# Sixteen phase-scaled copies of the values: from VectorE to GpSimd

## The chip, the cores and the metric

The kernel runs on one core of one Trainium2 chip. The metric is the time of one execution in device microseconds (us); where several runs are given, their median. The core has five engines that take their own instructions in their own order and wait for each other by semaphores: TensorE (PE, matrix products; its weight loads are listed apart as PEld), VectorE (DVE), ScalarE (ACT), GpSimd (POOL) and SyncE (SP, which here issues most of the DMAs).

## The reference, cut to what matters

A sequence of 2048 tokens of width 448 goes through two branches, and a gate mixes them.

```python
x = A_x                                         # 1 x 2048 x 448, bf16
g = sigmoid((x * gate_w).sum(-1, keepdims=True))
# branch a: attention with 16 heads of 28
q, k, v = split(x @ wqkv)
p = softmax(einsum("bhqd,bhkd->bhqk", q, k) * 28 ** -0.5)
a = merge(einsum("bhqk,bhkd->bhqd", p, v)) @ wo
# branch b: a filter in the two-dimensional spectrum
b = irfft2(rfft2(B_x) * (w_r + 1j * w_i))
out = g * a + (1 - g) * b
```

The change touches only the attention, and in it only the values that one part of the softmax weights is multiplied with.

## The kernel before, in words

The 16 heads are handled as four groups `g` of four heads. The 2048 queries are cut into four chunks `c` of 512, the 2048 keys into 16 tiles `kt` of 128. So there are 16 stages, one for each pair of a group and a chunk; their order is groups 0 and 1 chunk by chunk, then groups 2 and 3 in turn. In a stage, each key tile gives a score block of 128 keys by 512 queries for each of four heads, and the exponentials of that block have to be made and multiplied with the values.

There are two ways to the exponentials. Most key tiles go through ACT: PE writes the scores to `psA` or `psB`, ACT writes their exponential into `ring` (L1034), PE multiplies `ring` with the values `vw` into the accumulator `pvb`. The last three to five key tiles of a stage (two in the very first), 69 over the kernel, go another way, called d below: PE writes the scores to a `bg` bank, DVE adds a constant and writes 16-bit whole numbers whose bits, read as bf16, are close to the exponential (L993, four instructions for four heads, into one `pd` buffer). POOL makes three more versions of that buffer, each with another whole number added to all bits (L1003, INT64_ADD, one instruction for each version, into another `pd` buffer). The four versions are four phases of the same approximation, and their mean is a better exponential. PE multiplies each of the four with its own copy of the values, `vd`, and adds all of them into `pvb`. Nine `pd` buffers go round; a new version can only be written when PE has read what the buffer held.

The copies `vd` take out what the phases added: for each phase `f` the values of the tiles concerned, with a column of weights, are multiplied by the constant `PHGAIN[f]`. That is the line of this change. For each group the source is `vt` (f32, 20 blocks of 29 numbers on each partition, written by DVE at L879 and POOL at L826), and four instructions on L888 write the four copies in bf16, sixteen in all. They stand in `v_block`, and what reads them is listed in `vdready`. Each group has its copies made shortly ahead of its first stage; groups 0 and 2 share one `vd` buffer, groups 1 and 3 the other.

In the background of the attention PE, DVE and SP carry the spectral branch and the projections of the next groups.

The order of all this is no scheduler's choice at build time. Every piece of work is recorded as an operation with an engine, and a packed table (`TABLE`, unpacked in `Sched.run`) lists the operations in the order in which they are emitted. Each engine gets its own instructions in that order. The duration and due time that are given with an operation are not read when the order comes from the table.

Two more things bear on the lines touched. An operation of DVE that is recorded with `lk=True` is followed by a note (`ported`), and `pin` then makes the next GpSimd instruction wait for that DVE instruction. And the program that is built names, ahead of GpSimd instructions of some kinds, a library that these need: an instruction without a tile's name, shown as `ISA` in the order. In the kernel before there is one of these ahead of L1003, at the first INT64_ADD.

Of the kernel before, what the change touches and what calls it, by code (L numbers as in the profile page):

```python
# [21 lines left out]
S, D, H, DH, F = 2048, 448, 16, 28, 225  # L22
# [106 lines left out]
def free_dims(ap, dims, offset=0):  # L129
    return _AP(tensor=ap.tensor, offset=ap.offset + offset,  # L130
               ap=[list(ap.ap[0])] + [list(d) for d in dims])
# [16 lines left out]
def dv(n, rate=1):  # L148
    return 0.067 + n / 960.0 / rate
# [138 lines left out]
class Kernel:  # L288
# [544 lines left out]
    def v_block(self, g, b, due, wop, rel=0.0):  # L833
        self.sc.ctx = ("v_block", g, b)
        nc = self.nc
        it = Item()
        ops = []
        W = self.wv0 if g == 0 else self.wvr
        o0 = 0 if g == 0 else self.WV0[g]
        m = 113 if g == 0 else 112  # L840
        for t in range(4):
            for c in range(4):
                n = CH[c]

                def f(t=t, c=c, n=n):
                    self.mm(self.bgi(it)[:, m * t:m * t + m], self.xT[b][0:n, c, 128 * t:128 * t + 128],
                            W[0:n, c, o0:o0 + m], c == 0, c == 3)
                deps = [self.xev[b, cc] for cc in range(4)] + self.wvd[g] + [wop[0]]
                ops.append(self.pe(112, f, deps + ops[-1:], due - 1.5, dur=0.052, acq=it if not ops else None, rel=rel))
        last = []  # L850
        if g == 0:
            def fg():
                self.pin(nc.vector.tensor_copy(out=self.glog[:, 4 * b:4 * b + 4],
                                               in_=free_dims(self.bgi(it), [[m, 4]], 112)))
            last = [self.dve(0.08, fg, ops[-1:], due - 1.5)]
            self.glops.append(last[0])
        tl = range(4 * b, 4 * b + 4)
        nv = len([t for t in tl if any(t in self.ak[self.nidx[g, c]] for c in range(4))])
        dl = [t for t in tl if any(t in self.dk[self.nidx[g, c]] for c in range(4))]
        d0 = dl[0] if dl else None  # L860
        vr = [wop[1]]
        if nv:
            def fe():
                src = free_dims(self.bgi(it), [[m, nv], [DH, 4], [1, DH]])
                wv = free_dims(self.w[g][:], [[4, nv], [1, 4], [0, DH]], 16 * b)
                self.pin(nc.vector.tensor_tensor(out=free_dims(self.vw[g][:], [[128, nv], [32, 4], [1, DH]], 4 * b * 128),
                                                 in0=src, in1=wv, op=ALU.mult))
            last = [self.dve(dv(112 * nv), fe, [ops[-1], wop[0], self.vms[g], ("vwar", g)] + last, due - 1.5,
                             free=None if dl else it)]
            vr.append(last[0])  # L870
        nd = len(dl)
        if nd:
            o = d0 - NT + DKT

            def fd():
                src = free_dims(self.bgi(it), [[m, nd], [DH, 4], [1, DH]], m * (d0 - 4 * b))
                wv = free_dims(self.w[g][:], [[4, nd], [1, 4], [0, DH]], 4 * d0)
                dst = free_dims(self.vt[:], [[4 * (DH + 1), nd], [DH + 1, 4], [1, DH]], 4 * (DH + 1) * o)
                self.pin(nc.vector.tensor_tensor(out=dst, in0=src, in1=wv, op=ALU.mult))  # L879
            last = [self.dve(dv(112 * nd), fd, [ops[-1], wop[0]] + self.vtr + last, due - 1.4, free=it)]  # L880
            self.vtw.setdefault(g, []).extend([last[0]] + [self.vdw[g, t] for t in dl])
        if b == 3 and self.vtw.get(g):
            t0 = min(t for c in range(4) for t in self.dk[self.nidx[g, c]])
            n4, o4 = 4 * (NT - t0), t0 - NT + DKT
            rd = []
            for f in range(4):
                def fs(f=f):
                    self.pin(nc.vector.tensor_scalar(  # L888
                        out=free_dims(self.vd[g][:], [[32, n4], [1, DH + 1]], 128 * (DKT * f + o4)),
                        in0=free_dims(self.vt[:], [[DH + 1, n4], [1, DH + 1]], 4 * (DH + 1) * o4),  # L890
                        scalar1=PHGAIN[f], scalar2=None, op0=ALU.mult))
                rd.append(self.dve(dv(n4 * (DH + 1), 2), fs, [self.vdms[g], ("vdwar", g)] + self.vtw[g], due - 1.3, lk=True))
            self.vtr = rd
            for t in range(t0, NT):
                self.vdready[g, t] = [[x] for x in rd]
        self.vready[g, b] = vr
# [574 lines left out]
```

## Time and profile before

| | |
|---|---|
| time, median of 3 runs | 380.67 us (380.51 to 381.52) |
| the profiled execution | 380.98 us |
| its span | 379.2 us |
| PE busy | 371.3 us (98%) |
| ACT busy | 351.1 us (93%) |
| DVE busy | 339.1 us (89%) |
| POOL busy | 234.4 us (62%) |

The profile is of one execution. A row of a group of instructions gives the line, the engine, the operation, the output and the input by the names in the program without buffer numbers, and how often it ran; then the busy time and the mean of one; then how long the engine stood idle just before them and what ended that. A row of a timeline gives the start, the length, the same names, and in brackets the idle time ahead of it and what released it. Rows whose engine ends in q (POOLq, SPq) are of the engine's own sequencer: waits, DMA issues, settings. Busy times of PE are partly modelled, so that 98% isn't PE at its peak.

### The profile page before, as it was taken

The page shows a single profiled execution, that of the slowest core. Times are in us where ns is not written, and L with a number is a line of the kernel's source. Part 1 is how long each engine was busy: PE and PEld are TensorE (multiplying, and loading weights), DVE is VectorE, ACT ScalarE, POOL GpSimd, SP SyncE. Part 2 cuts the span into 40 slices and gives each one's busy share as a digit, 9 for nine tenths or more (in the row PEclk, how much of TensorE's full clock was granted, in tenths as well). Part 3 has the DMA queues.
Part 4 walks back from the last instruction along what each step waited for, and adds up shares of the span by engine and source line. Part 5 has one row for each costly group of instructions (what it writes and reads, how often), then busy time and mean ns, then how long its engine had stood idle before and what let it go on. Part 6 is the DMA issues. An engine that isn't in the chain of part 4 may idle for free.

```text
span 379.2 us, 12643 instructions
## 1 busy us (share of the span) xinstructions
PE 371.3 (98%) x5117; PEld 142.4 (38%) x5117; DVE 339.1 (89%) x665; ACT 351.1 (93%) x389; POOL 234.4 (62%) x264
## 2 busy tenths in 40 slices
PE   8999999999999999999999999999999999999996
PEld 6634223342433333234333434233333323433564
DVE  1768899999999999999999999999999999988744
ACT  2799999999999999999999999999999999999841
POOL 4446465866778866565553565778597778483510
PEclk9999999999999999999999999999999999999999
DMA  6511101010210112211322212223222122222132
GB/s 145 157 34 44 29 18 36 4 36 2 41 52 22 44 41 54 55 38 30 68 60 93 69 40 49 57 61 70 45 64 74 30 69 72 86 64 72 35 103 75
DMA packets 31158, 21.23 MB, mean 56 GB/s; under 512 B 16260, under 2 KB 29052, under 8 KB 31100
## 3 DMA queue, kind: packets, MB, share of 16 engines
q1 hardware_dynamic: 29708, 19.96, 20.7%
q8 instruction: 40, 0.66, 0.7%
q10 hardware_dynamic: 1392, 0.46, 0.5%
q14 instruction: 18, 0.15, 0.1%
HBM read 14.51 MB, written 1.96 MB: 43 GB/s over the span
## 4 chain that ended last, share of the span: by engine, by line
PE 55%; ACT 31%; issue 6%; DVE 4%; DMA 2%; POOL 1%; SPq 0%; DVEq 0%; ACTq 0%; POOLq 0%
ACT ring L1034 31%; PE bg L432 24%; PE pvb L432 17%; PE psA L432 7%; PE psB L432 6%; DVE pd L993 2%; PE bg L435 1%; DMA CS<-cCS 1%; DVE X L1419 1%; POOL pd L1003 1%; DMA Wg<-in_B_w_i_dram 0%; DVE X L1298 0%; DVE q L1178 0%; DVE t L1362 0%; DVE wpq L1224 0%
## 5 line engine op out<-in xcount | busy, mean ns | idle before, releaser
L1003 POOL INT64_ADD pd<-pd x207 | 211.9, 1038 | 96.7 <-DVE pd L993 27.4
L1034 ACT ACTIVATE ring<-psA 128x1024 bf16<-128x1024 f32 x187 | 201.7, 1078 | 4.7 <-PE psA L432 3.2
L1034 ACT ACTIVATE ring<-psB 128x1024 bf16<-128x1024 f32 x187 | 201.7, 1079 | 2.6 <-PE psA L432 1.4
L993 DVE TENSOR_SCALAR pd<-bg 128x512 uint16<-128x512 f32 x276 | 180.9, 681 | 8.5 <-PE bg L432 3.5
L432 PE MATMUL pvb<-pd,vd 128*32 128x512 bf16 x1104 | 96.9, 384 | 0.1
L432 PE MATMUL bg<-q,k 32*128 32x512 bf16 x276 | 96.3, 383 | 0.2
L432 PEld LDWEIGHTS <-k 32*128 32x128 bf16 x1024 | 40.1, 91 | 122.4 <-issue 117.7
L432 PE MATMUL psB<-q,k 32*128 32x512 bf16 x374 | 73.2, 383 | 1.3 <-ACT ring L1034 0.7
L432 PE MATMUL psA<-q,k 32*128 32x512 bf16 x374 | 72.8, 383 | 0.5 <-ACT ring L1034 0.2
L432 PE MATMUL pvb<-ring,vw 128*32 128x512 bf16 x748 | 67.9, 384 | 0.0
L432 PEld LDWEIGHTS <-vd 128*32 128x32 bf16 x1104 | 25.3, 94 | 35.5 <-issue 31.1
L432 PEld LDWEIGHTS <-vw 128*32 128x32 bf16 x748 | 17.5, 94 | 22.7 <-issue 20.5
L432 PEld LDWEIGHTS <-xT 128*128 128x128 bf16 (+5 forms) x512 | 20.3, 97 | 10.7 <-issue 9.7
L432 PE MATMUL bg<-xT,wpq 128*32 128x512 bf16 (+3 forms) x244 | 21.2, 383 | 0.1
L1362 DVE TENSOR_TENSOR t<-bg,Wg 128x450 bf16<-128x450 f32 x32 | 18.8, 614 | 0.6 <-DMA Wg<-in_B_w_i_dram 0.4
L432 PE MATMUL bg<-xT,wpk 128*32 128x512 bf16 (+2 forms) x240 | 18.9, 383 | 0.0
L432 PE MATMUL bg<-wvr,xT 128*128 128x112 bf16 (+2 forms) x192 | 13.7, 213 | 0.0
L1178 DVE TENSOR_TENSOR q<-pvs,Rb 128x512 bf16<-128x512 f32 x15 | 10.9, 729 | 2.6 <-DMA Rb<-rsc 2.6
L1298 DVE TENSOR_TENSOR X<-bg,oc 128x226 bf16<-128x226 f32 (+1 forms) x32 | 12.3, 386 | 0.5
L432 PEld LDWEIGHTS <-CS 128*32 128x32 bf16 x384 | 9.0, 95 | 9.9 <-issue 5.6
L432 PE MATMUL bg<-xtok,CS 128*32 128x225 bf16 (+1 forms) x192 | 11.2, 294 | 0.7 <-DMA CS<-cCS 0.7
L742 DVE TENSOR_SCALAR k<-bg 128x512 bf16<-128x512 f32 x15 | 10.3, 685 | 1.3 <-PE bg L432 1.1
(117 smaller groups left out, 315.4 us busy)
## 6 DMA issues: line engine op xcount, KB each, us to landing
Rb<-rsc SPq DMA_DIRECT2D x60, 64.0 KB
CS<-cCS SPq DMA_DIRECT2D x16, 192.0 KB
V<-xtok SPq DMA_DIRECT2D x16, 113.0 KB
Wg<-in_B_w_i_dram SPq DMA_DIRECT2D x64, 28.1 KB
xtok<-Ab SPq DMA_DIRECT2D x16, 112.5 KB
xtok<-in_A_x_dram SPq DMA_DIRECT2D x3, 448.0 KB
Wg<-in_B_w_r_dram SPq DMA_DIRECT2D x32, 28.1 KB
out_dram<-wpq SPq DMA_DIRECT2D x6, 112.0 KB
```

The source lines that it names most:

```text
L432: self.pin(self.nc.tensor.matmul(out, lhsT=lhsT, rhs=rhs, start=start, stop=stop, **kw))
L435: self.pin(self.nc.tensor.transpose(out=out, in_=in_, identity=self.c("ident")[0:n, 0:n]))
L742: self.pin(nc.vector.tensor_scalar(out=dst, in0=self.bgi(it), scalar1=SQ, scalar2=None, op0=ALU.mult))
L993: self.pin(nc.vector.tensor_scalar(out=ys[:, s, :].bitcast(U16), in0=self.bgi(it), scalar1=127 * UNITS, scalar2=0.0, op0=ALU.add, op1=ALU. ...
L1003: self.pin(nc.gpsimd.int64_add(out=fl(pds), in0=fl(ys), in1=PHASE[f] * 0x0001000100010001))
L1034: self.pin(nc.scalar.activation(out=self.ring[:, u0:u0 + len(st), :], in_=slot[:, 0:len(st), :], func=ACT.Exp, scale=LN2 / UNITS))
L1178: e = self.dve(dv(512), lambda: self.pin(nc.vector.tensor_tensor(out=dst, in0=pvs[:], in1=self.Rb[:], op=ALU.mult)), ds, kk, lk=True)
L1298: self.pin(nc.vector.tensor_tensor(out=free_dims(self.X1[:, t, :], [[F, 2], [-1 if dif else 1, n]], (F - 1) * dif), in0=free_dims(self.bgi ...
L1362: self.pin(nc.vector.tensor_tensor(out=out[:], in0=self.bgi(it)[:, 0:F2].rearrange("p (a f) -> p a f", a=2), in1=free_dims(Wg[:], [[F, 2], ...
L1419: self.pin(nc.vector.tensor_tensor(out=free_dims(self.zt[0:FN], [[128, 4], [1, 128]], 512 * t), in0=self.bgi(it)[0:FN, :].rearrange("p (a ...
```

## The change

The sixteen instructions on L888 are issued on GpSimd in place of VectorE. They are recorded with a duration of 0.9 in place of one worked out for VectorE, and without the note that makes the next GpSimd instruction wait for them. The table of the order is the same, so each of the sixteen stands at the same place in the common order and therefore at a place in GpSimd's queue that the table gave to it for VectorE.

```diff
             for f in range(4):
                 def fs(f=f):
-                    self.pin(nc.vector.tensor_scalar(
+                    self.pin(nc.gpsimd.tensor_scalar(
                         out=free_dims(self.vd[g][:], [[32, n4], [1, DH + 1]], 128 * (DKT * f + o4)),
                         in0=free_dims(self.vt[:], [[DH + 1, n4], [1, DH + 1]], 4 * (DH + 1) * o4),
                         scalar1=PHGAIN[f], scalar2=None, op0=ALU.mult))
-                rd.append(self.dve(dv(n4 * (DH + 1), 2), fs, [self.vdms[g], ("vdwar", g)] + self.vtw[g], due - 1.3, lk=True))
+                rd.append(self.pool(0.9, fs, [self.vdms[g], ("vdwar", g)] + self.vtw[g], due - 1.3))
```

Three pieces of the order show what this does to the queues. In them a name such as `pd_113` is a tile with its number, `x2` means that two such instructions follow each other, and `L1003 ISA` with tiles is the INT64_ADD. An `ISA` without tiles sets the library: in the built program the one at L888 names library 0, the one at L1003 library 1.

GpSimd, at the copies of group 0, shortly before PE first reads them:

```order
 L533 COPY wpk_79<-X_131 96x8x28
-L1003 ISA pd_113<-pd_111 128x1024
+L888 ISA
+L888 TENSOR_SCALAR vd_116<-vt 128x20x29 x2
+L1003 ISA
+L1003 ISA pd_113<-pd_111 128x1024
+L888 ISA
+L888 TENSOR_SCALAR vd_116<-vt 128x20x29 x2
+L1003 ISA
 L1003 ISA pd_114<-pd_111 128x1024
```

Four copies came into the queue in two pairs with one INT64_ADD between them, and four settings of the library with them.

GpSimd, at the copies of group 3, whose first stage is the tenth:

```order
 L1003 ISA pd_113<-pd_110 128x1024
-L1003 ISA pd_111<-pd_110 128x1024
-L1003 ISA pd_107<-pd_115 128x1024
+L888 ISA
+L888 TENSOR_SCALAR vd_117<-vt 128x20x29 x3
+L1003 ISA
+L1003 ISA pd_111<-pd_110 128x1024
+L1003 ISA pd_107<-pd_115 128x1024
+L888 ISA
+L888 TENSOR_SCALAR vd_117<-vt 128x20x29
+L1003 ISA
 L1003 ISA pd_107<-pd_114 128x1024
```

Three copies and one, with two INT64_ADD between them. Over the kernel there are nine such clusters (two for group 0, three for group 1, two each for groups 2 and 3), and each brings one setting to library 0 and one back to library 1: eighteen more than before. In one cluster of group 1 a small cast (`vw`, L817) stands between the copy and the way back.

VectorE, at the copies of group 0:

```order
 L993 TENSOR_SCALAR pd_115<-bg_64 128x512
-L888 TENSOR_SCALAR vd_116<-vt 128x20x29
 L903 TENSOR_SCALAR ge<-ge 128x16
 L993 TENSOR_SCALAR pd_115<-bg_66 128x512
-L888 TENSOR_SCALAR vd_116<-vt 128x20x29
 L993 TENSOR_SCALAR pd_115<-bg_64 128x512
 L742 TENSOR_SCALAR k_89<-bg_65 128x512
-L888 TENSOR_SCALAR vd_116<-vt 128x20x29 x2
 L993 TENSOR_SCALAR pd_115<-bg_64 128x512
```

The copies left VectorE's queue and the rest closed up. The order of PE, ACT and SP is the same in both programs.

## The prediction

> **What bounds the kernel now.** I read the page first, then who waits for the lines touched, then the places in the trace where GpSimd would get its new work.
>
> ```profile
> PE 371.3 (98%) x5117; PEld 142.4 (38%) x5117; DVE 339.1 (89%) x665; ACT 351.1 (93%) x389; POOL 234.4 (62%) x264
> PE 55%; ACT 31%; issue 6%; DVE 4%; DMA 2%; POOL 1%; SPq 0%; DVEq 0%; ACTq 0%; POOLq 0%
> L1003 POOL INT64_ADD pd<-pd x207 | 211.9, 1038 | 96.7 <-DVE pd L993 27.4 <-PE pvb L432 12.6 <-PE psA L432 9.3
> ```
>
> PE and ACT feed each other without a gap and carry 86% of the chain that ended last. POOL has 1% of it and stands idle for 38% of the span. That suggests room on POOL, but the share is a mean; what counts is how far ahead of PE each INT64_ADD is done. I paired the 207 INT64_ADD with the products that read their buffers (by the buffers' numbers in the order). At the places concerned it looks like this, POOL's instruction first, then its reader:
>
> ```profile
> 48.44 5.10 POOL L1003 INT64_ADD pd<-pd  x5 [1.48 <-DVE pd L993]
> L432 PE MATMUL pvb<-pd,vd x4: 379/379/379, 50.7 to 50.7; 128*32 128x512 bf16 x4
> 105.09 1.04 POOL L1003 INT64_ADD pd<-pd  x1 [0.27 <-PE bg L432]
> L432 PE MATMUL pvb<-pd,vd x8: 379/384/390, 106.6 to 106.8; 128*32 128x512 bf16 x8
> 219.51 4.08 POOL L1003 INT64_ADD pd<-pd  x4 [0.40 <-PE pvb L432]
> L432 PE MATMUL pvb<-pd,vd x8: 379/379/379, 221.8 to 222.0; 128*32 128x512 bf16 x8
> 237.00 2.05 POOL L1003 INT64_ADD pd<-pd  x2 [0.86 <-PE pvb L432]
> L432 PE MATMUL pvb<-pd,vd x4: 389/390/390, 239.9 to 239.9; 128*32 128x512 bf16 x4
> ```
>
> One INT64_ADD takes 1.04 us. The first of the five at 48.44 is done at 49.48 and read at 50.7: a lead of 1.2 us. At 105.09 it is 0.7 us (read by the last four products, 106.8), at 219.51 1.45 us (222.0), at 237.00 1.9 us. So POOL is just in time. PE takes its instructions in a fixed order, so a late buffer stops not one product but everything behind it, the scores for ACT included; PE, 98% busy, has nothing to catch up with. Delay of POOL beyond idle time and lead goes into the time one for one.
>
> **The change part by part.**
>
> *Removed from VectorE.* Sixteen instructions of 0.47 us.
>
> ```profile
> L888 DVE TENSOR_SCALAR vd<-vt x16: 398/454/645, 38.5 to 236.2; 128x580 bf16<-128x580 f32 x16
>   POOL pd L1003: 8.2, 5
>   POOL vw L817: 2.5, 1
> ```
>
> Between them they are 7.2 us of VectorE. The two rows under the first list who waited for them: only POOL, 10.7 us in six places; those waits go with the notes. PE and ACT never waited for them, and L888 isn't in the chain. Ends: a gain of 7.2 us and nothing; I take nothing, since VectorE has 4% of the chain and POOL, not VectorE, is what these places will wait for.
>
> *Added to GpSimd: the copies.* No row has this operation there. The nearest are of other kinds:
>
> ```profile
> L661 POOL MEMSET vd<- 128x2560 bf16 x2 | 4.5, 2231 | 1.4 <-DVE sq L747 1.4
> 17.77 0.25 POOL L817 CAST vw<-w 128x16 bf16<-128x16 f32 x1
> 104.35 0.46 POOL L817 CAST vw<-w 128x64 bf16<-128x64 f32 x1 [2.53 <-DVE vd L888]
> 14.16 0.37 POOL L530 COPY wpq<-X 128x224 bf16<-128x224 bf16 x1 [2.39 <-DMA X<-in_A_wqkv_dram]
> ```
>
> The memset makes 0.87 ns an element; the two casts, which write scattered elements, differ by 0.21 us for 48 elements, 4.4 ns each. So 580 elements cost between 0.5 and 2.7 us. The copy with 224 elements in runs of 28 is nearest in layout (the new one has runs of 29): with a fixed part of 0.18 us, what the small cast has beyond its 16 elements, it makes 0.85 ns an element, and 580 come to 0.67 us. Sixteen: 10.7 us (the high end adds 33).
>
> *Added to GpSimd: eighteen changes of library.* This is the large term, and the trace before shows one such change:
>
> ```profile
> L1003 POOLq MODIFY_POOL_CONFIG  x2: 1/1/1, 32.5 to 32.5; - x2
> 32.06 0.37 POOL L626 MEMSET wvr<- 1x336 bf16 x1
> 33.27 1.04 POOL L1003 INT64_ADD pd<-pd  x1 [0.83 <-DVE pd L993]
> DMA packets 0, 0.00 MB, mean 0 GB/s; under 512 B 0, under 2 KB 0, under 8 KB 0
> ```
>
> Two records at 32.5 us, and the first INT64_ADD starts 0.83 us after the memset, a gap that is put down to VectorE. So here a change costs between nothing and 0.83 us. But the last row, of the stretch 32.4 to 33.3 us, says that no byte was moved meanwhile. Every earlier execution ended with this same library in use, so perhaps nothing had to change. In the changed kernel each of the eighteen names the other library than the one in use. If its code has to come from memory, the nearest rows are loads from memory that an engine stood waiting for, and the one row in which an engine takes in a table:
>
> ```profile
> 1.17 2.78 ACTq L407 DMA_DIRECT2D X<-in_A_wqkv_dram  x4
> 4.87 0.21 DVE L533 COPY wpq<-X 96x224 bf16<-96x224 bf16 x1 [4.87 <-DMA X<-in_A_wqkv_dram]
> 10.47 1.24 SPq L407 DMA_DIRECT2D X<-in_A_wqkv_dram  x2
> 3.98 1.28 ACT L575 ACT_TABLE_LOAD   x1 [3.98 <-issue]
> ```
>
> From the start of the issue to the reader's start: 1.17 to 4.87, and 10.47 to POOL's 14.16 (quoted above), both times 3.7 us. A change that is a load and then an installing costs 3.7 + 1.3 = 5.0 us, an estimate; two loads in series, one for each of the two records, 7.4 us. Ends: 0 and 7.4. I take 5.0, since a change that really changes something is nearer to a load than to the row in which no byte moved.
>
> The Trainium skill (GPSIMD Engine Reference, Instruction dispatch) says that the first call to a freshly loaded kernel also pays a load of about 6 us, measured between this same record and the first instruction behind it, without an instruction in the profile. The row at 32.5 us disagrees, with 0.83 us at most; by 5.95 us a change the sum below would be 492 us.
>
> *What hides it.* POOL's idle time at the nine places. The windows are those ahead of the clusters of group 0 (two), group 1 (the first), and groups 2 and 3 whole:
>
> ```profile
> 38.59:40.51 1.92, 1.92 (x27) 0.60 (x22) 1.60 (x5) 1.92 (x3) 0.00 (x0) 1.00 0.27 98
> 41.55:42.70 1.15, 1.15 (x19) 0.25 (x11) 1.15 (x4) 1.15 (x3) 0.00 (x1) 1.00 0.00 0
> 101.83:104.35 2.52, 2.52 (x36) 0.96 (x34) 2.52 (x8) 2.52 (x4) 0.00 (x0) 1.00 0.18 37
> 211.45:215.79 4.34, 4.31 (x62) 1.88 (x59) 4.34 (x12) 4.34 (x6) 1.04 (x1) 1.00 0.35 78
> 232.17:237.00 4.83, 4.81 (x65) 1.43 (x57) 4.80 (x12) 4.83 (x7) 2.05 (x2) 1.00 0.15 29
> sum 14.76, PE 14.70 PEld 5.12 DVE 14.40 ACT 14.76 POOL 3.09; mean PE 2.94 PEld 1.02 DVE 2.88 ACT 2.95 POOL 0.62
> 113.44 2.05 POOL L1003 INT64_ADD pd<-pd  x2 [1.10 <-DVE vd L888]
> 116.98 2.05 POOL L1003 INT64_ADD pd<-pd  x2 [1.08 <-DVE pd L993]
> ```
>
> That is 14.76 - 3.09 = 11.7 us, and in group 1 another 0.27 (at 105.09), 1.10 and 1.08: 14.1 us. The leads above can be used up once for each group: 5.2 us. Behind a late POOL the next wait is PE's for `pvb<-pd,vd`, and behind PE ACT's for `psA` and `psB`.
>
> The sum: 18 x p + 10.7 - 14.1 - 5.2 = 18 x p - 8.6, with p the price of one change; 5.0 gives 81 us.
>
> *PE after a stall.* Nine stalls of some 81 / 9 = 9 us each. Before, PE never stops that long, so the price of a restart is bounded by its first microseconds:
>
> ```profile
> 1.10 4.24 PE L432 MATMUL bg<-zero 128*128 128x256 bf16 x19 [1.10 <-POOL zero L509]
> 7.24 0.81 PE L432 MATMUL bg<-xT,wpq 128*128 128x512 bf16 x3
> ```
>
> At first 256 columns take 0.21 us (19 starts within 4.24 less one length of 0.42); from 7.24 on 512 columns take 0.21 us. So PE begins at half speed for at most 6 us and loses at most 2.8 us. Nine times: 0 to 25 us. I take the middle, 13, since nothing before shows whether a stall of 9 us brings the slow start back. The Trainium skill (TensorE: Matmul & The Clock Gate, Part 1) says that an idle window of about 3.4 us does, and that as long of activity ends it; at half speed that is 1.7 us a stall, 15 us in place of 13.
>
> **Result.** 380.98 us (span 379.2, 1.8 around it; 0.3 above the median 380.67) + 81 + 13 = 475 us.
>
> **Rivals.** *Cheap changes (0.8 to 1.3 us).* For it: the one change shown has a gap of 0.83 us; if a change costs what the table load does, 1.28. Against it: nothing was moved there. 18 x 0.83 - 8.6 = 6 us, 18 x 1.28 - 8.6 = 14: 387 to 395 us, without PE's restarts, as the stalls are too short.
>
> *Not slower.* If a change is only its two records, the copies alone, 10.7 us, fit in the 14.1 us of idle time that they inherit, and the note's waits are gone. It decides at p = 8.6 / 18 = 0.48 us: below that the time stays 381, or falls by up to 1 us if VectorE's relief reaches the chain. Against it: eighteen changes at 0.48 us or less need both libraries to lie ready beside each other.
>
> *Dear changes.* Two loads in series, 7.4 us: 18 x 7.4 - 8.6 + 25 = 150, 531 us. For it: two records for each change. Or copies at 2.7 us each.
>
> **How the numbers follow.** The forecast, that each change is a real load, has 0.62, with a range of its own from 439 us (3.7 us, no slow restarts) to 505 (6 us, all of them). Cheap changes 0.20, not slower 0.08, dear 0.10. The range 386 to 508 leaves out the last two. A measurement of this kernel can tell about 0.3% from no change: faster 0.03, within it 0.05, slower 0.92.
>
> **What would show it.** Eighteen more pairs of MODIFY_POOL_CONFIG; behind each a gap on POOL of about 5 us, in which it waits for nothing shown; nine stretches around 40, 105 to 120, 215 and 237 us with PE and ACT idle; L888 on POOL at about 0.67 us; outside of these stretches, the same lengths as before. The prediction is wrong if the gaps behind the records are under 1.3 us, or if PE runs on during them.

## The result, and the profile after

The changed kernel takes 511.2 us (median of 3 runs, 510.55 to 514.49) where the kernel before takes 380.67 us: 1.345 times as long (95% interval 1.341 to 1.349). The direction was forecast, the size was not: 475 us, with a range that ended at 508. The profiled execution took 510.55 us, 129.6 us more than the one before.

The page of the changed kernel, busy time of the engines, the rows of 40 slices for PE, POOL and PE's clock, the chain, and the groups touched:

```profile
span 508.8 us, 12680 instructions
PE 396.4 (78%) x5117; PEld 144.4 (28%) x5117; DVE 337.2 (66%) x649; ACT 355.7 (70%) x389; POOL 261.1 (51%) x280
PE   8993099999471629999999307952399999999997
POOL 5452156759242258656543225342287688776520
PEclk9997569999866659999999756575689999999999
PE 55%; issue 19%; POOL 11%; ACT 7%; DVE 6%; DMA 1%; SPq 0%; POOLq 0%; DVEq 0%; ACTq 0%
L1003 POOL INT64_ADD pd<-pd x207 | 211.8, 1036 | 139.9 <-issue 46.8
L432 PE MATMUL pvb<-pd,vd 128*32 128x512 bf16 x1104 | 107.4, 421 | 105.2 <-POOL vd L888 57.2
L888 POOL TENSOR_SCALAR vd<-vt 128x580 bf16<-128x580 f32 x16 | 26.9, 1684 | 62.7 <-issue 55.1
```

POOL's share of the chain went from 1% to 11%, and "issue" from 6% to 19%: time in which an engine waits for nothing that the profile shows. On POOL such time stands ahead of the two lines that a change of library precedes: 55.1 us ahead of L888, 46.8 us ahead of L1003. PE now stands ahead of `pvb<-pd,vd` for 105.2 us; the same row of the kernel before has 0.1 us in that place:

```profile
L432 PE MATMUL pvb<-pd,vd 128*32 128x512 bf16 x1104 | 96.9, 384 | 0.1
```

In the row of the slices of the changed kernel PE shows the places, the slices around 45 to 65, 130 to 190, 285 to 310 and 335 to 370 us: the four groups. Elsewhere PE is as full as before.

The first of these places in POOL's timeline, and the same stretch on PE:

```profile
38.20 0.37 POOL L533 COPY wpk<-X 96x224 bf16<-96x224 bf16 x1
45.48 3.44 POOL L888 TENSOR_SCALAR vd<-vt 128x580 bf16<-128x580 f32 x2 [6.91 <-issue]
54.76 1.03 POOL L1003 INT64_ADD pd<-pd  x1 [5.83 <-issue]
62.53 3.44 POOL L888 TENSOR_SCALAR vd<-vt 128x580 bf16<-128x580 f32 x2 [6.74 <-issue]
71.81 2.05 POOL L1003 INT64_ADD pd<-pd  x2 [5.83 <-issue]
```

```profile
47.24 0.62 PE L432 MATMUL pvb<-pd,vd 128*32 128x512 bf16 x4 [4.94 <-POOL vd L888]
64.29 0.62 PE L432 MATMUL pvb<-pd,vd 128*32 128x512 bf16 x4 [16.43 <-POOL vd L888]
```

Over the kernel each way to library 0 leaves a gap of 6.7 to 7.1 us on POOL, each way back 5.7 to 6.0 us; typical values are 6.9 and 5.85. Each pair of copies takes 3.44 us. PE waits 4.94 us for the first copy and 16.43 us for the next that it needs, which stands behind a way back, an INT64_ADD and another way there. The instructions behind which the gaps stand are nearly nothing themselves:

```profile
L888 POOLq MODIFY_POOL_CONFIG  x18: 1/7/11, 38.5 to 352.4; - x18
L888 POOL TENSOR_SCALAR vd<-vt x16: 1660/1702/1702, 45.5 to 359.5; 128x580 bf16<-128x580 f32 x16
```

Eighteen records of 1 to 11 ns on L888 (two for each of nine changes), and twenty on L1003, of which two were there before.

### The profile page after: what moved, and what is told of

The parts are those of the page before. It is cut to its first block, busy times and chain, and to the rows that moved or that the text cites. A ratio compares the mean times of both kernels' runs of the same rounds, so it can differ in the third digit from the quotient of the medians.

```text
span 508.8 us, 12680 instructions
## 1 busy us (share of the span) xinstructions
PE 396.4 (78%) x5117; PEld 144.4 (28%) x5117; DVE 337.2 (66%) x649; ACT 355.7 (70%) x389; POOL 261.1 (51%) x280
## 4 chain that ended last, share of the span: by engine, by line
PE 55%; issue 19%; POOL 11%; ACT 7%; DVE 6%; DMA 1%; SPq 0%; POOLq 0%; DVEq 0%; ACTq 0%
PE bg L432 21%; PE pvb L432 19%; PE psB L432 7%; PE psA L432 7%; ACT ring L1034 7%; POOL pd L1003 6%; POOL vd L888 5%; DVE pd L993 3%; PE bg L435 1%; DVE t L1362 1%; DMA Wg<-in_B_w_i_dram 1%; DMA CS<-cCS 1%; DVE X L1298 1%; SPq L407 0%; DVE q L1178 0%
## 5 line engine op out<-in xcount | busy, mean ns | idle before, releaser
L1003 POOL INT64_ADD pd<-pd x207 | 211.8, 1036 | 139.9 <-issue 46.8
L1034 ACT ACTIVATE ring<-psA 128x1024 bf16<-128x1024 f32 x187 | 198.9, 1064 | 72.5 <-PE psA L432 56.1
L1034 ACT ACTIVATE ring<-psB 128x1024 bf16<-128x1024 f32 x187 | 199.1, 1065 | 59.8 <-PE bg L432 37.0
L432 PE MATMUL pvb<-pd,vd 128*32 128x512 bf16 x1104 | 107.4, 421 | 105.2 <-POOL vd L888 57.2
L432 PE MATMUL bg<-q,k 32*128 32x512 bf16 x276 | 102.8, 409 | 0.3
L432 PE MATMUL psB<-q,k 32*128 32x512 bf16 x374 | 77.6, 405 | 1.2 <-ACT ring L1034 0.7
L432 PE MATMUL psA<-q,k 32*128 32x512 bf16 x374 | 76.6, 403 | 0.2
L432 PE MATMUL pvb<-ring,vw 128*32 128x512 bf16 x748 | 71.3, 403 | 0.0
L888 POOL TENSOR_SCALAR vd<-vt 128x580 bf16<-128x580 f32 x16 | 26.9, 1684 | 62.7 <-issue 55.1
L742 DVE TENSOR_SCALAR q<-bg 128x512 bf16<-128x512 f32 x15 | 10.2, 678 | 24.2 <-PE bg L432 24.2
L1315 DVE CAST Ab<-bg 128x450 bf16<-128x450 f32 x16 | 9.8, 619 | 15.5 <-PE bg L432 15.5
L432 PE MATMUL bg<-wvr,xT 128*128 128x112 bf16 (+2 forms) x192 | 14.1, 217 | 0.0
```

Of the source, the lines that this page charges most:

```text
L432: self.pin(self.nc.tensor.matmul(out, lhsT=lhsT, rhs=rhs, start=start, stop=stop, **kw))
L742: self.pin(nc.vector.tensor_scalar(out=dst, in0=self.bgi(it), scalar1=SQ, scalar2=None, op0=ALU.mult))
L888: self.pin(nc.gpsimd.tensor_scalar(out=free_dims(self.vd[g][:], [[32, n4], [1, DH + 1]], 128 * (DKT * f + o4)), in0=free_dims(self.vt[:], ...
L1003: self.pin(nc.gpsimd.int64_add(out=fl(pds), in0=fl(ys), in1=PHASE[f] * 0x0001000100010001))
L1034: self.pin(nc.scalar.activation(out=self.ring[:, u0:u0 + len(st), :], in_=slot[:, 0:len(st), :], func=ACT.Exp, scale=LN2 / UNITS))
L1315: e = self.dve(.54, lambda: self.pin(nc.vector.tensor_copy(out=ab[:], in_=self.bgi(it2)[:, 0:F2])), [m, ard[t % 3]], k2, free=it2)
```

## The experiments

Theory: the changes of library are the cost, by stopping POOL for 6.9 or 5.85 us each. Rivals: the copies themselves, on an engine that is just in time; and PE's slow restarts behind the stalls.

**No change of library at all.** The factor is left out, so the copies aren't scaled.

```diff
-                    self.pin(nc.gpsimd.tensor_scalar(
+                    self.pin(nc.gpsimd.tensor_copy(
                         out=free_dims(self.vd[g][:], ...),
-                        in0=free_dims(self.vt[:], ...),
-                        scalar1=PHGAIN[f], scalar2=None, op0=ALU.mult))
+                        in_=free_dims(self.vt[:], ...)))
```

> The sixteen operations stay on GpSimd at the same places, but as plain copies: the factor PHGAIN is left out, and with it every change of library. Theory (the eighteen changes are the cost): only 16 copies of 0.7 to 1.7 us are left, 11 to 27 us against 19 us of idle time and leads, so 380 to 390 us. Rival (moving the work itself to GpSimd is the cost: GpSimd is just in time and VectorE hinders it): well over 400 us.

Measured: 381.42 us beside 381.39 us for the kernel before on the same chip, ratio 1.0005 (0.999 to 1.002). It has the two records of a change that the kernel before has, and no more. A line of its page and one of its groups on POOL:

```profile
PE 371.2 (98%) x5117; PEld 142.2 (37%) x5117; DVE 335.1 (88%) x649; ACT 351.0 (92%) x389; POOL 244.8 (65%) x280
L888 POOL CAST vd<-vt 128x580 bf16<-128x580 f32 x16 | 10.5, 680 | 2.7 <-DVE q L1177 1.5 <-DVE vt L879 0.5 <-DVE ge L906 0.5
```

Sixteen instructions of the same shape and at the same places, 0.68 us each, cost nothing that can be told from noise: 10.5 us of work went into idle time. VectorE had 4 us less to do (335.1 for 339.1), and that gained nothing. Moving work of this size to POOL is free in itself; what isn't free is the kind of instruction.

**The changes without the copies.** To the kernel before, with its copies on VectorE, a multiplication of one number on each partition (128x1) is added on GpSimd behind each copy.

```diff
         def f():
+            self.tiny = None
             fn()
             self.port = self.cur
+            if self.tiny:
+                self.tiny()
...
+                    self.tiny = lambda: self.pin(nc.gpsimd.tensor_scalar(
+                        out=self.one[:], in0=self.one[:], scalar1=1.0, scalar2=None, op0=ALU.mult))
```

> The copies are back on VectorE as before. Behind each of them GpSimd multiplies one number on each partition of a tile that nothing reads; that brings the same eighteen changes of library at the same places. Theory: 18 x 6.3 us (the gaps measured in the changed kernel) less 19 us, 95 us, and restarts of PE of 10 to 26 us: 485 to 500 us. Rival (the copies at 1.7 us each are the cost): under 400 us.

Measured: 494.49 us, ratio 1.298 (1.294 to 1.301), 113 us more than before. It has the same 38 records of changes as the changed kernel. Two of POOL's groups in this kernel:

```profile
L1010 POOL INT64_ADD pd<-pd x207 | 212.2, 1040 | 143.1 <-issue 52.6 <-DVE pd L1000 30.2 <-PE pvb L436 11.5
L897 POOL TENSOR_SCALAR one<-one 128x1 f32<-128x1 f32 x16 | 3.8, 238 | 66.5 <-issue 44.2 <-DVE pd L1000 14.7 <-DVE X L1305 7.1
```

Sixteen instructions of 0.24 us, 3.8 us in all, and nearly the whole loss: 113 of 130 us. So the changes are the main cost. By difference 17 us are left for the copies as they are (26.9 us on POOL). From the two lengths of the same operation, 0.24 us for one element and 1.68 us for 580, an estimate of 2.5 ns an element follows; the plain copy of the run above took 0.68 us for the 580.

**Fewer changes.** The first try put all four copies of a group at the place of phase 0, though other phases come first in the order, so that some products read copies that were not yet written.

```diff
-                def fs(f=f):
-                    self.pin(nc.gpsimd.tensor_scalar(
+                def fs(f0=f):
+                  for f in range(4) if f0 == 0 else ():
+                    self.pin(nc.gpsimd.tensor_scalar(
```

> The four copies of each group are issued one behind the other at the place of the first, so there are eight changes of library in place of eighteen, and the copies are the same. Theory: 8 x 6.3 + 16 x 1.75 - 19 = 59 us and a restart of PE of up to 2.8 us in each of four places: 440 to 452 us. Rival (the cost goes with the copies, not with the changes): about 511 us, as the changed kernel.

Measured: 454.15 us, ratio 1.191 (1.185 to 1.198). The second try puts them at the place of whichever comes first, so that nothing is read early.

```diff
+        self.made = set()
...
-                def fs(f=f):
-                    self.pin(nc.gpsimd.tensor_scalar(
+                def fs(g=g, n4=n4, o4=o4):
+                  todo, self.made = (() if g in self.made else range(4)), self.made | {g}
+                  for f in todo:
+                    self.pin(nc.gpsimd.tensor_scalar(
```

> As the run with eight changes, but the four copies of a group stand at the place of whichever of them comes first in the order, so that every product reads finished copies. Theory: 8 x 6.4 us + 28 us of copies, less 12 us that the changed kernel turned out to hide: 448 us (440 to 458). Rival (the cost goes with the copies): about 511 us.

Measured: 455.24 us, ratio 1.195 (1.192 to 1.198). Ten changes fewer, the same sixteen copies, 56 us less: 5.6 us for each change, with whatever hides a part of it taken off. The rival by which the cost goes with the copies falls; it wanted 511. The first try came out 2 us above its bounds, the second within them.

**One group alone.**

```diff
-                    self.pin(nc.gpsimd.tensor_scalar(
+                    self.pin((nc.gpsimd if g == 1 else nc.vector).tensor_scalar(
...
-                rd.append(self.pool(0.9, fs, ...))
+                rd.append(self.pool(0.9, fs if g == 1 else self.ported(fs), ...))
```

> Only the copies of group 1 are on GpSimd, four copies in three clusters with six changes; the other twelve stay on VectorE with their notes. Theory (the delays of the clusters add up): 6 x 6.4 + 4 x 1.75 less 3 us, 42 us, a time of 423 us (415 to 428). Rival (one group's delay is caught up later, the cost grows faster than the number of clusters): under 410 us.

Measured: 425.11 us, ratio 1.116 (1.113 to 1.118), 44 us for six changes and four copies. The delays add up; nothing is caught up.

**PE kept busy through the stalls.** Ahead of eleven products of the changed kernel PE adds products of zeros into the accumulator.

```diff
             if c < FILL0:
+                for _ in range(KEEP.get(self.ops[c].tag[0], 0)):
+                    self.keep()
                 self.ops[c].emit()
...
+KEEP = {("pv", 0, "d", 14, 1): 40, ("pv", 0, "d", 14, 2): 148, ...}
...
+        self.sc.keep = lambda: self.mm(self.pv[:, 0:256], self.zero[:, 0:P], self.zero[:], False, False)
```

> The changed kernel, and ahead of the eleven products at which PE stood still for 3 us and more, PE multiplies zeros (858 products of 256 columns, made long enough to end about 0.7 us before each stall did) into the accumulator. Theory (half speed after each stall costs what PE's busy time grew by, 25 us): 485 us. Rival (GpSimd is late in any case and the slow restart lies beside it): 505 to 515 us.

Measured: 513.2 us, ratio 1.346 (1.339 to 1.353), the same as the changed kernel's 1.345. Two lines of its page:

```profile
PE 485.5 (95%) x5975; PEld 229.0 (45%) x5975; DVE 336.0 (66%) x649; ACT 355.6 (70%) x389; POOL 262.0 (51%) x280
PEclk9999989999999988999999998559999999999999
```

The added products did only a part of what they should. The mean granted clock rose from 0.862 to 0.960, but the kernel's own products still ran at half speed for 35.5 us (68.2 to 71.6, 187.6 to 194.5 and 313.9 to 344.6 us), where the changed kernel had 57 us. The longest stretch of this run, and the one of the changed kernel around the same products (start and end; length, then the busy time of PE, PEld, DVE, ACT and POOL with their instructions; granted clock, DMA share, GB/s):

```profile
313.90:344.60 30.70, 29.16 (x208) 9.91 (x208) 14.24 (x30) 16.39 (x16) 14.76 (x15) 0.50 0.13 32
313.70:330.80 17.10, 16.15 (x129) 3.74 (x121) 9.48 (x19) 9.60 (x10) 8.45 (x9) 0.50 0.07 18
```

In the changed kernel PE stands still for only 0.95 us of its 17.10, yet its products, set beside the same products of the kernel before, go from 93.6 to 101.4 us late there. Nine of the eleven products behind the additions keep their distance from the POOL instruction that they wait for; one starts 0.45 us later, and one, at the end of the longer stretch, 4.3 us later. And the eighteen gaps of the changes add up to 117.0 us in this run, for 114.7 in the changed kernel.

So the time of this run doesn't show that the half speed, 25 us by PE's busy time (396.4 for 371.3), costs nothing. What the two traces show goes by place. Behind the second cluster of group 1 this run has the full clock and gains nothing by it: from there to the product that waits for the third cluster it loses 0.65 us, as much as the change to library 0 in between is longer (7.72 us for 7.07). POOL is late there in any case, and a faster PE only waits sooner. Between the first and the second cluster of group 1 POOL waits for PE (2.16 and 0.92 us in the changed kernel, 0.46 here), and there the full clock gained 2.4 us. Behind the last stall of groups 1 and 2 PE's lateness grew at half speed with hardly a wait, and this run didn't lift the half speed there.

**Why the kernel before paid nothing for its one change.** Behind everything else on POOL one multiplication was added to the kernel before, so that each execution ends with library 0 in use.

```diff
         self.sc.run(self.filler)
+        self.pin(self.nc.gpsimd.tensor_scalar(out=self.one[:], in0=self.one[:], scalar1=1.0, scalar2=None, op0=ALU.mult))
```

> The kernel before, and behind everything else on GpSimd one multiplication of one number on each partition, which needs library 0. So each execution leaves library 0 in use, and the one change at 32.5 us, to library 1, has something to change. Theory (a change is free only if the library is in use already, and it stays in use from one execution to the next): the gap ahead of the first INT64_ADD is 5.7 us in place of 0.83, and the time 381 to 385 us, as the first buffers had leads of 6.6 us and more. Rival (the first change of an execution is cheap for another reason): gap 0.83 us, 381 us.

Measured: 389.21 us, ratio 1.023 (1.020 to 1.025). POOL's timeline at the first change and at the added one:

```profile
31.87 0.37 POOL L629 MEMSET wvr<- 1x336 bf16 x1
38.03 1.03 POOL L1006 INT64_ADD pd<-pd  x1 [5.79 <-DVE vt L882]
...
374.99 0.26 POOL L328 TENSOR_SCALAR one<-one 128x1 f32<-128x1 f32 x1 [6.84 <-DVE wpq L1227]
```

The same instruction at the same place, with the same code around it, now has a gap of 5.79 us in place of 0.83. But for a memset of one number on each partition, all that differs ahead of it is which library the execution before left in use. A change to the library that is in use already is nearly free (0.83 us at most), and the library stays in use from one execution to the next; the row of the kernel before showed this case and no other. (The gap is put down to VectorE because a wait for it stands there; that wait was over at 32.9 us.) The gap is as expected, the time is not: the kernel as a whole lost 6.5 us in the profiled executions and 8 us in the medians, for a first INT64_ADD that was 4.8 us late; the end of POOL's own queue, at 375.3 of 385.7 us, isn't what ends it. The trace shows where the rest of the profiled execution went. Two groups of products in the kernel before, then the same two in this one, and between these two a stretch of this run:

```profile
42.23 0.61 PE L432 MATMUL pvb<-pd,vd 128*32 128x512 bf16 x8
45.61 0.39 PE L432 MATMUL psB<-q,k 32*128 32x512 bf16 x2
46.72 1.05 PE L434 MATMUL pvb<-pd,vd 128*32 128x512 bf16 x8
52.40 0.39 PE L434 MATMUL psB<-q,k 32*128 32x512 bf16 x2
46.50:52.00 5.50, 5.50 (x43) 1.04 (x44) 2.33 (x5) 3.20 (x4) 2.06 (x2) 0.50 0.01 3
```

PE is 4.5 us late at the first group and 6.8 us at the second, though it never stops in between: its clock is 0.50. So the restart behind this one stall cost 2.3 us. The other 1.7 us of the medians stay open.

## Why the prediction was right or wrong

The mechanism was right: each change really changed something and stopped POOL. The forecast failed at two terms of its sum, the price of a change (5.0 us, measured 6.4) and the length of a copy (0.67 us, measured 1.68).

*Right: what bounds, and where it would show.* POOL was just in time, PE's order is fixed, and what POOL lost beyond idle time and leads went into the time. The listed signs came, but for the length of the copies: eighteen pairs of records, gaps behind each in which POOL waits for nothing shown, PE and ACT idle around 40, 105 to 120, 215 and 237 us of the old time, and elsewhere the same lengths, but for PE's half speed behind the stalls. That VectorE's relief would gain nothing, and that sixteen copies of 0.68 us fit in the idle time they inherit, was shown by the run without changes.

*Right in kind, too low in size (a step that failed): the price of a change.* The 5.0 us came from a load of 3.7 us and an installing of 1.3. Measured are 6.9 us to library 0 and 5.85 us to library 1, a mean of 6.4: 9 x 6.9 + 9 x 5.85 = 115 us in place of 90. The Trainium skill (GPSIMD Engine Reference, Instruction dispatch) gives about 6 us for the load behind this record at the first call to a freshly loaded kernel. The changed kernel agrees, with 5.83 us from the end of the copies to the first INT64_ADD at 54.76, and each of its eighteen changes took 5.7 to 7.1 us, not only a first. Where the prediction held the row at 32.5 us against that rule, the rule was right and the row was of a change that changed nothing.

*Right conclusion from a wrong reason.* The prediction concluded from a row without DMA traffic that nothing was loaded at 32.5 us. That nothing had to change is borne out by the run that ends on library 0. But the row proves nothing. This is the same view of the changed kernel from 49.2 to 54.7 us, within a change that took 5.8 us:

```profile
DMA packets 0, 0.00 MB, mean 0 GB/s; under 512 B 0, under 2 KB 0, under 8 KB 0
```

If code is brought in during that time, this view doesn't show it; what POOL does in the gap is not shown by any run.

*Wrong (a step that failed): the copies.* The step took the row of a plain copy, 0.67 us. As a plain copy the instruction did take 0.68. But a multiplication is not a copy: 1.68 us each, 26.9 us in place of 10.7. The upper end of the bounds, 2.7 us, had held it. The mistake was to let a row with the same layout stand for another operation, when no row before had a multiplication on POOL.

*About right, as far as can be told: what hides it, and PE's restarts.* The sum counted 14.1 us of idle time and 5.2 us of leads as cover, and 13 us for restarts: 6 us of cover net. In the changed kernel 115 + 26.9 - 129.6 = 12 us were covered net of restarts. No run separates the two; the trace allows an estimate. Behind the last stalls of groups 1, 2 and 3 PE goes on at half speed (187.1 to 190.8, 313.7 to 330.8, 368.3 to 371.7 us) and becomes 1.6, 6.9 and 1.4 us later (0.95 us of waits taken off), 10 us in all; with the 2.4 us between the first clusters of group 1 it is 12. With these, the cover would be 22 to 25 us beside the 19.3 counted. The run with group 1 alone agrees: 3 x 6.9 + 3 x 5.85 + 4 x 1.7 = 45 us of work and 3.7 us at half speed behind its last stall (159.9 to 168.5 us, PE busy throughout) cost 44, so 5 us were covered, or 7 with those 2.4, where the same count gives 5.7.

The way to the 13 us was in part luck: nine equal restarts were assumed, and the traces show some that another wait absorbs and one of 6.9 us. The slow clock is real, as the rule on idle windows of the Trainium skill (TensorE: Matmul & The Clock Gate, Part 1) says and the row of the clock shows (down to 0.5 of full speed in the slices of the stalls). That 3.4 us of activity end it, as the prediction took from there, this trace doesn't bear out: from 313.7 on the clock stayed at 0.50 for 17.10 us, with PE busy for 16.15 of them.

Put together: 94 us were forecast and 129.6 measured. The changes add 25, the copies 16, and 6 us more were covered net of restarts: 94 + 25 + 16 - 6 = 129. The range ended 3 us too low because it was drawn around the price of a change and left the upper end of the copies to a rival that was left out.

## What to carry to other kernels

Before an instruction is moved to GpSimd, look in the built program for what it brings along: here each change between two kinds of instructions stopped the engine for six to seven microseconds, and the number of changes, set by the order, decided most of the cost, not the work that was moved. A price read from the only instance in a trace may be that of the case in which nothing had to be done; ask what state the execution before left behind. An engine that is idle for a third of the time can still be the one that the others wait for within a microsecond, and then its gaps, not its busy time, count. When an experiment is meant to remove a cost, see in its trace whether the cost is gone: the run with PE kept busy still had most of the half speed where it counts.

## What the runs showed of the hardware that was not expected

- The way to library 0 (6.7 to 7.1 us in the changed kernel) takes about 1 us longer than the way to library 1 (5.7 to 6.0 us).
- GpSimd's library outlives an execution: with the same program around it the first change takes 0.83 us or 5.79 us, by what was in use when the execution before ended.
- On GpSimd a multiplication of f32 by a constant into bf16 takes 1.68 us for 580 elements on each partition, a plain copy with the same operands 0.68 us.
- PE's clock can stay at half speed while PE is busy: 0.50 for 17.10 us of the changed kernel with PE busy for 16.15 of them. In the run that ends on library 0 one stall of 4.5 us brought 2.3 us more by half speed.
